# Exponentials written to the scores' PSUM bank, and scores issued after the previous pair's values and transposes

## The chip, the cores and the metric

One core of a Trainium2 chip. The metric is device time in microseconds, the median of several executions. TensorE is PE, VectorE DVE, ScalarE ACT, GpSimd POOL and SyncE SP.

## The reference

Windowed attention feeds two feed-forward blocks. q, k and v have 4 batches, 8 heads, 576 positions and 64 per head:

```python
scores = scale * np.matmul(q, k.transpose(0, 1, 3, 2))
mask = (rel >= 0) & (rel < 64)
scores = np.where(mask, scores, -1000000000.0)
attn = np.exp(scores - np.max(scores, axis=-1, keepdims=True))
attn = attn / (np.sum(attn, axis=-1, keepdims=True) + 1e-09)
x = np.matmul(attn, v)             # 2304 tokens x 512
a, b = x @ w1, x @ w2              # 512 -> 1024 each
x = (a * b @ w3) @ w_out           # -> 512
h = x @ w_in                       # 512 -> 2048
out = (h * sigmoid(h)) @ w_out2    # -> 512
```

q, k, v and the output are float32, the weights float64.

## The kernel before, in words

The kernel has three parts. The weight stage (`phase_w`, to 92 us) converts the 64-bit weights to float32 in pieces of 128x512 and multiplies w3 and w_out into one matrix (L582). A piece passes through two steps on ACT (L125, L128), two on DVE (L138, whose result `cv_z` lies in PSUM, and L141), an addition on POOL (L145), and for some a split in a high and a low part (L153 on ACT, L157 on DVE or POOL). `phase_a` runs once for each of six blocks of 384 tokens: 24 units of 12 matmuls (L618, L648), whose sums ACT copies (L632) and DVE multiplies (L634), and whose product is split again (L85, L88). The last part, from about 400 us on, is the second feed-forward block; the change does not touch it.

Attention is cut into 72 steps, here called pairs: two heads by 128 tokens. Each pair is laid over the work of the other parts in halves. `half(h)` is called between the matmuls of the weight stage (28 halves) and then once per unit of `phase_a`. Pair g goes through four even and odd halves:

- even half 2g: `scores(g)` puts the scores of both heads, 128x2x192, in one PSUM bank (tag "s", one buffer). DVE adds the mask, scales and reduces them (L344, once per head), to `sm` in SBUF. ACT then takes the exponentials (`exps`, L355, once per head) with their sums.
- odd half 2g+1: `normalise(g)` reduces the sums (L363), inverts them (L365) and multiplies (L367), all on DVE.
- even half 2g+2: `transposes(g)` (L377, three on PE into the bank "t") and their copy or split by `split_t` (L383, or L387 to L392).
- even half 2g+4: `values(g)` (L404 to L406, or L411 and L412) into the bank "o"; the parts are added in the following odd half (L419 to L423).

Pairs below 17 are "plain": one float32 matmul for scores (L329), and one copy each for transposes and values (L383, L407). The others work with high and low parts (L333, L337, L297, L303, L309, L318, L321).

Everything is in program order on each engine (the schedule is written by hand): what stands first in an engine's stream waits, and all behind it waits too. `fill()` puts steps of the weight conversion between attention's DVE instructions, so both share one queue.

The bank "s" is free for the next pair, in the kernel before, as soon as both L344 have read it. `sm` has two buffers.

Of the kernel before, what the change touches and what calls it, by code (L numbers as in the profile page):

```python
# [13 lines left out]
AF = mybir.ActivationFunctionType  # L14
ALU = mybir.AluOpType
# [27 lines left out]
def tile_window_attention_ffn(ctx, tc, qkv, qkp, vp, mask, w1, w2, w3t, w_out, w_in, w_out2, out):  # L43
# [7 lines left out]
    nc = tc.nc  # L51
# [189 lines left out]
    NG = NU * NPAIR  # L241
    LAST_HALF = 2 * NG + 4
    qk_raw, v_raw, qk_st, v_st, s_st, p_st = {}, {}, {}, {}, {}, {}
# [17 lines left out]
    def plain(g):  # L261


        return g < PLAIN
# [59 lines left out]
    def scores(g):  # L324
        s_ps = psa.tile([128, 2, 192], F32, name=f"s{g}", tag="s")
        t = qk_raw.pop(g) if plain(g) else qk_st.pop(g)
        if plain(g):
            k = t.rearrange("p (h n) -> p h n", h=2)[:, :, 0:192]
            nc.tensor.matmul(s_ps, lhsT=t[:, 192:320], rhs=k, start=True, stop=True)  # L329
        else:  # L330
            for h in range(2):

                nc.tensor.matmul(  # L333
                    s_ps[:, h], lhsT=t[:, 128 + h * 128 : 256 + h * 128],
                    rhs=t[:, 384 + h * 192 : 576 + h * 192], start=(h == 0), stop=False,
                )
            nc.tensor.matmul(s_ps, lhsT=t[:, 0:128], rhs=k_lo[g % 2], start=False, stop=True)  # L337
        nm = att.tile([128, 2], F32, name=f"nm{g}", tag="nm", bufs=2)
        rs = att.tile([128, 2], F32, name=f"rs{g}", tag="rs", bufs=2)
        fill(2)  # L340
        at = mask_at[mask_kind(place(g)[0])]
        for h in range(2):

            nc.vector.tensor_tensor_reduce(  # L344
                out=sm[g % 2][:, h, :], in0=s_ps[:, h, :], in1=consts[:, at + 64 - 64 * h : at + 256 - 64 * h],
                op0=ALU.add, op1=ALU.min, scale=-(D ** -0.5), scalar=3.0e38, accum_out=nm[:, h : h + 1],
            )
        fill()
        s_st[g] = (nm, rs)

    def exps(g):
        nm, rs = s_st[g]
        for h in range(2):
            x = sm[g % 2][:, h, :]
            nc.scalar.activation(  # L355
                out=x, in_=x, func=AF.Exp, scale=-1.0, bias=nm[:, h : h + 1], accum_out=sums_of[g % 2][:, h, 0:1]
            )

    def normalise(g):
        _, rs = s_st.pop(g)  # L360
        x = sm[g % 2]
        fill()
        nc.vector.tensor_reduce(out=rs, in_=sums_of[g % 2], axis=mybir.AxisListType.X, op=ALU.add)  # L363
        fill()
        nc.vector.reciprocal(out=rs, in_=rs)  # L365
        fill()
        nc.vector.tensor_tensor(out=x, in0=x, in1=rs.unsqueeze(2).to_broadcast([128, 2, 192]), op=ALU.mult)  # L367

    def transposes(g):

# [9 lines left out]
    def split_t(g, t_ps):  # L380
        if plain(g):
            p_st[g] = p_w[g % 2]
            nc.scalar.copy(out=p_st[g], in_=t_ps[:, 0:320])  # L383
            return
        b, a = pt[g % 2, 1], pt[g % 2, 0]
        own, before = t_ps[:, 0:256].rearrange("p (h n) -> p h n", h=2), t_ps[:, 256:320]
        nc.scalar.copy(out=b[:, :, 0, :], in_=own)  # L387
        for h, hs in HEADS:
            nc.scalar.copy(out=a[hs, h, 0], in_=before[hs])
        nc.vector.tensor_tensor(out=b[:, :, 1, :], in0=own, in1=f32(b[:, :, 0, :]), op=ALU.subtract)  # L390
        for h, hs in HEADS:
            nc.vector.tensor_tensor(out=a[hs, h, 1], in0=before[hs], in1=f32(a[hs, h, 0]), op=ALU.subtract)  # L392

    def values(g):
        u, c = place(g)
        r = u % 3 * 128

        tag = "z" if done["step"] == len(line) and g % 2 else "o"
        o_ps = psa.tile([128, 2, 2, 128], F32, name=f"o{g}", tag=tag)
        if plain(g):  # L400


            v, p, o = v_p[g % 3], p_st.pop(g), o_ps[:, 0, 0]
            nc.tensor.matmul(o, lhsT=v[:, 0:128], rhs=p[:, 0:128], start=True, stop=False)  # L404
            nc.tensor.matmul(o, lhsT=v[:, 64:192], rhs=p[:, 128:256], start=False, stop=False)
            nc.tensor.matmul(o[:, 0:64], lhsT=v[:, 192:320], rhs=p[:, 256:320], start=False, stop=True)  # L406
            return lambda: nc.scalar.copy(out=xr[:, c, r : r + 128], in_=o)  # L407
        vhl = v_st.pop(g)
        b, a = pt[g % 2, 1], pt[g % 2, 0]
        for h in range(2):  # L410
            nc.tensor.matmul(o_ps[:, h], lhsT=vhl[:, h], rhs=b[:, h], start=(h == 0), stop=False)  # L411
        nc.tensor.matmul(o_ps[:, :, :, 0:64], lhsT=vhl[:, 2], rhs=a, start=False, stop=True)  # L412
        o_ps = o_ps.rearrange("p h t n -> p h (t n)")

        def total():
            t = att.tile([128, 256], F32, name=f"ot{g}", tag="ot", bufs=1)
            if g == NG - 1:
                att.tile([128, 24], F32, name="odd_end", tag="odd_end", bufs=1)
            nc.scalar.copy(out=t[0:64], in_=o_ps[64:128, 0, :])  # L419
            nc.scalar.copy(out=t[64:128], in_=o_ps[0:64, 1, :])  # L420
            nc.vector.tensor_tensor(out=t[0:64], in0=o_ps[0:64, 0, :], in1=t[0:64], op=ALU.add)
            nc.vector.tensor_tensor(out=t[64:128], in0=o_ps[64:128, 1, :], in1=t[64:128], op=ALU.add)  # L422
            nc.gpsimd.tensor_tensor(out=xr[:, c, r : r + 128], in0=t[:, 0:128], in1=t[:, 128:256], op=ALU.add)  # L423

        return total

    def half(h):

        g, odd = divmod(h, 2)
        if not odd:
            if g < NG:
                scores(g)
            squeeze(unit_of[0])
            if 2 <= g <= NG + 1:
                sums.append(values(g - 2))
                if plain(g - 2):
                    sums.pop()()
            if 1 <= g <= NG:  # L440
                split_t(g - 1, transposes(g - 1))
            if g < NG:
                exps(g)
        else:
            if g < NG:
                normalise(g)
            if sums:
                sums.pop()()
            lows = prep_qk(g + 2)
            if g < NG:  # L450
                lows += prep_v(g)
            blk, r = divmod(g - 2, 3 * NPAIR)
            if r == 3 * NPAIR - 1 and not plain(g - 2):
                split_x(blk, 3)
            for low in lows:
                low()

            for x in range(g + 2, g + 5):
                if plain(x) and x > g + 2:
                    break  # L460
                load_qk(x)
            for x in range(g + 1, g + 4):
                if g < (x - 1 if plain(x - 3) else x - 3):
                    break
                load_v(x)
# [675 lines left out]
```

## Time and profile before

| | |
|---|---|
| median of 3 executions | 841.4 us (841.26 to 842.33) |
| profiled execution, its time | 841.24 us |
| its span | 839.5 us |
| PE, DVE, ACT, POOL busy | 827.4, 615.3, 561.2, 529.7 us |
| TensorE clock granted | 1.0 throughout |

The span is the time between the first and the last instruction that the profile shows; 1.7 us of the execution lie around it. A busy time is the sum of an engine's instructions, so an engine at 99% can have few gaps, and one at 70% can still be the one that others wait for in a stretch. The timeline gives start and duration of each instruction on each engine; "[0.71 <-DVE sm L367]" behind a row says how long the engine was idle before it and who ended that.

### The profile page before, as it was taken

The numbers are of one execution on the slowest core, as the hardware profiler recorded it, in microseconds if no ns is written. First come the engines' busy times: TensorE is split into PE (matmuls) and PEld (weight loads), VectorE is DVE, ScalarE is ACT, GpSimd is POOL, SyncE is SP. The second block draws the span as 40 slices with busy tenths as digits, with TensorE's granted clock in tenths as the row PEclk, the third lists the DMA queues.
The fourth block names the chain that finished last, engine by engine and source line by source line (L and its number), as shares of the span: only waits on it lengthen the run. The fifth ranks groups of instructions, "written<-read, shape, count | busy, mean of one in ns | idle before, by whom it ended". The sixth has DMA issues, their size and how long they took to land.

```text
span 839.5 us, 14173 instructions
## 1 busy us (share of the span) xinstructions
PE 827.4 (99%) x4418; PEld 745.9 (89%) x4418; DVE 615.3 (73%) x1424; ACT 561.2 (67%) x1390; POOL 529.7 (63%) x588
## 2 busy tenths in 40 slices
PE   7999999999999999999999999999999999999998
PEld 3555799999999999999999988888888888988986
DVE  7889877688888888888368698998644567644544
ACT  6889778898898898898556566556543446443433
POOL 5768666677777677677565577876454456454441
PEclk9999999999999999999999999999999999999999
DMA  9998234444544544543433522301301201201002
GB/s 320 330 321 279 72 107 128 149 127 133 167 150 142 169 156 145 170 157 103 155 134 120 194 76 76 125 26 51 102 26 56 95 26 64 88 25 51 1 1 75
DMA packets 54682, 102.66 MB, mean 122 GB/s; under 512 B 5200, under 2 KB 32592, under 8 KB 54608
## 3 DMA queue, kind: packets, MB, share of 16 engines
q1 hardware_dynamic: 51008, 96.91, 35.5%
q10 hardware_dynamic: 3600, 4.85, 1.6%
q8 instruction: 35, 0.57, 0.3%
q14 instruction: 39, 0.32, 0.1%
HBM read 88.11 MB, written 13.63 MB: 121 GB/s over the span
## 4 chain that ended last, share of the span: by engine, by line
PE 69%; POOL 8%; ACT 6%; issue 4%; DVE 1%; ACTq 0%; POOLq 0%; DVEq 0%
PE o L882 24%; PE ab L618 14%; PE hy L828 12%; PE hx L828 9%; PE x L648 6%; POOL klo L303 2%; POOL vhl L321 1%; ACT sm L355 1%; PE t L377 1%; POOL xr L423 1%; ACT qkhi L297 1%; POOL p L88 1%; POOL cv_b L189 1%; PE o L411 1%; PE s L333 1%
## 5 line engine op out<-in xcount | busy, mean ns | idle before, releaser
L882 PE MATMUL o<-hl,gp 128*128 128x512 f32 x504 | 133.3, 394 | 0.0
L618 PE MATMUL ab<-xa,hl 128*128 128x384 f32 x576 | 119.0, 341 | 0.0
L828 PE MATMUL hy<-xop,j 128*128 128x384 f32 x576 | 115.9, 335 | 0.0
L618 PE MATMUL ab<-xb,hl 128*128 128x384 f32 x570 | 115.2, 334 | 0.0
L88 POOL TENSOR_TENSOR gp<-tmp,gp 128x384 fp32r<-128x384 f32 x56 | 64.1, 1145 | 77.5 <-ACT gp L85 75.9
L828 PEld LDWEIGHTS hy<-xop,j 128*128 128x128 f32 x576 | 102.6, 188 | 9.0 <-DVE tmp L722 1.0
L882 PEld LDWEIGHTS o<-hl,gp 128*128 128x128 f32 x504 | 93.1, 188 | 13.1
L618 PEld LDWEIGHTS ab<-xb,hl 128*128 128x128 f32 x570 | 100.3, 188 | 0.0
L618 PEld LDWEIGHTS ab<-xa,hl 128*128 128x128 f32 x576 | 99.1, 188 | 0.0
L844 ACT ACTIVATE tmp<-hx 128x384 f32<-128x384 f32 x48 | 23.6, 492 | 111.5 <-DVE hx L722 67.8
L722 DVE TENSOR_TENSOR tmp<-hy,tmp 128x384 f32<-128x384 f32 x96 | 53.2, 554 | 56.1 <-PE hy L828 51.5
L828 PE MATMUL hx<-xop,j 128*128 128x384 f32 x432 | 86.6, 335 | 0.0
L882 PE MATMUL o<-hl,gq 128*128 128x512 f32 x324 | 85.9, 393 | 0.0
L88 POOL TENSOR_TENSOR gq<-tmp,gq 128x384 fp32r<-128x384 f32 x36 | 39.0, 1084 | 74.3 <-ACT gq L85 74.3
L828 PEld LDWEIGHTS hx<-xop,j 128*128 128x128 f32 x432 | 76.8, 188 | 4.1
L423 POOL TENSOR_TENSOR xr<-ot 128x128 f32<-128x128 f32 x55 | 32.7, 594 | 73.7 <-DVE ot L422 65.5
L303 POOL TENSOR_TENSOR klo<-qk,qkhi 64x192 fp32r<-64x192 f32 x110 | 67.2, 611 | 7.6 <-ACT qkhi L297 2.7
L882 PEld LDWEIGHTS o<-hl,gq 128*128 128x128 f32 x324 | 60.3, 188 | 11.2
L648 PE MATMUL x<-p,wp 128*128 128x384 f32 x360 | 69.6, 339 | 0.0
L355 ACT ACTIVATE sm<-sm,nm 128x192 f32<-128x192 f32 x144 | 64.5, 450 | 3.9 <-DVE nm L344 2.5
L648 PEld LDWEIGHTS x<-p,wp 128*128 128x128 f32 x360 | 61.9, 188 | 0.0
L145 POOL TENSOR_TENSOR cv_b<-cv_b,cv_r 128x512 int32<-128x512 int32 x32 | 48.6, 1520 | 18.8 <-DVE cv_b L141 9.4
(146 smaller groups left out, 1896.7 us busy)
## 6 DMA issues: line engine op xcount, KB each, us to landing
qk<-in_qkv SPq DMA_DIRECT2D x55, 384.0 KB, 3.1
words<-in_w_out SPq DMA_DIRECT2D x24, 512.0 KB, 5.4
r<-w_in SPq DMA_DIRECT2D x22, 512.0 KB, 3.4
words<-in_w3t SPq DMA_DIRECT2D x16, 512.0 KB, 6.5
words<-in_w SPq DMA_DIRECT2D x16, 512.0 KB, 6.2
xe<-in_w_in SPq DMA_DIRECT2D x16, 512.0 KB, 4.8
v<-in_qkv SPq DMA_DIRECT2D x55, 96.0 KB, 2.7
x2d<-x2s ACTq DMA_DIRECT2D x24, 192.0 KB, 1.9
```

The lines of the kernel that those rows point to most:

```text
L88: (nc.vector if eng_lo == "dve" else nc.gpsimd).tensor_tensor(out=lo, in0=src, in1=f32(hi), op=ALU.subtract)
L145: nc.gpsimd.tensor_tensor(out=x, in0=b, in1=self.r, op=ALU.add)
L189: nc.gpsimd.tensor_tensor(out=self.b, in0=self.b, in1=self.r, op=ALU.add)
L303: nc.gpsimd.tensor_tensor(out=k_lo[g % 2][hs, h * 192 : h * 192 + 192], in0=t[hs, n], in1=f32(hi[hs, n]), op=ALU.subtract)
L355: nc.scalar.activation(out=x, in_=x, func=AF.Exp, scale=-1.0, bias=nm[:, h : h + 1], accum_out=sums_of[g % 2][:, h, 0:1])
L423: nc.gpsimd.tensor_tensor(out=xr[:, c, r : r + 128], in0=t[:, 0:128], in1=t[:, 128:256], op=ALU.add)
L618: nc.tensor.matmul(acc, lhsT=w[:, l, fs], rhs=x[k // 2][:, k % 2, r, :], start=(k == 0 and n == 0), stop=(k == 3 and n == 2),)
L648: nc.tensor.matmul(acc, lhsT=wp[f][:, l, o * 128 : (o + 1) * 128], rhs=p[f][:, r, :], start=(f == 0 and n == 0), stop=(f == 7 and n == 2),)
L722: eng.tensor_tensor(out=out, in0=a, in1=b, op=op)
L828: nc.tensor.matmul(bank[name], lhsT=w[:, l, at + kt], rhs=x[:, kt, r, :], start=(fresh and kt == 0 and n == 0), stop=(kt == 1 and n == 2), ...
L844: nc.scalar.activation(out=sg, in_=src, func=AF.Sigmoid)
L882: nc.tensor.matmul(oacc[t], lhsT=g[:, l, cols], rhs=weights["out", 2 * p + i][:, r, :], start=(p == 0 and i == 0 and n == 0), stop=(p == P ...
```

## The change

`exps` writes its result to the PSUM tile of the scores, `s_ps`, in place of `sm`, and `normalise` reads it from there and writes `sm` as before. The bank "s" is thus in use until normalise has read it. So that the next pair's scores can be issued after that, an even half now has `values(g-2)`, then `transposes(g-1)`, then `scores(g)`, where it had the scores first. The calls that follow on ACT and DVE keep their order.

```diff
         fill()
-        s_st[g] = (nm, rs)
+        s_st[g] = (nm, rs, s_ps)
 
     def exps(g):
-        nm, rs = s_st[g]
+        nm, rs, e = s_st[g]
         for h in range(2):
             x = sm[g % 2][:, h, :]
             nc.scalar.activation(
-                out=x, in_=x, func=AF.Exp, scale=-1.0, bias=nm[:, h : h + 1], accum_out=sums_of[g % 2][:, h, 0:1]
+                out=e[:, h, :], in_=x, func=AF.Exp, scale=-1.0, bias=nm[:, h : h + 1], accum_out=sums_of[g % 2][:, h, 0:1]
             )
...
-        _, rs = s_st.pop(g)
+        _, rs, e = s_st.pop(g)
...
-        nc.vector.tensor_tensor(out=x, in0=x, in1=rs.unsqueeze(2).to_broadcast([128, 2, 192]), op=ALU.mult)
+        nc.vector.tensor_tensor(out=x, in0=e, in1=rs.unsqueeze(2).to_broadcast([128, 2, 192]), op=ALU.mult)
...
         if not odd:
+            if 2 <= g <= NG + 1:
+                sums.append(values(g - 2))
+            t_ps = transposes(g - 1) if 1 <= g <= NG else None
             if g < NG:
                 scores(g)
             squeeze(unit_of[0])
-            if 2 <= g <= NG + 1:
-                sums.append(values(g - 2))
-                if plain(g - 2):
-                    sums.pop()()
-            if 1 <= g <= NG:
-                split_t(g - 1, transposes(g - 1))
+            if sums and plain(g - 2):
+                sums.pop()()
+            if t_ps:
+                split_t(g - 1, t_ps)
             if g < NG:
                 exps(g)
```

PE's stream around even half 20 in the weight stage, before (s10 are the scores of pair 10, o8 and t9 the values and transposes of the pairs before it, accw the weight product):

```order
L582 MATMUL accw1_1_588<-wo_94,q_95 128x512
L329 MATMUL s10_711<-kq0_81 128x384
L404 MATMUL o8_721<-pw0_96,vp2_85 128x128
L405 MATMUL o8_721<-pw0_96,vp2_85 128x128
L406 MATMUL o8_721<-pw0_96,vp2_85 128x64
L377 MATMUL t9_726<-consts_69,sm1_78 128x128 x3
L582 MATMUL accw1_2_589<-wo_94,q_95 128x512
```

and in the change, whose lines from 435 on have a number that is higher by one:

```order
L583 MATMUL accw1_1_588<-wo_94,q_95 128x512
L404 MATMUL o8_711<-pw0_96,vp2_85 128x128
L405 MATMUL o8_711<-pw0_96,vp2_85 128x128
L406 MATMUL o8_711<-pw0_96,vp2_85 128x64
L377 MATMUL t9_715<-consts_69,sm1_78 128x128 x3
L329 MATMUL s10_719<-kq0_81 128x384
L583 MATMUL accw1_2_589<-wo_94,q_95 128x512
```

The scores moved behind the values and the transposes; all else stands where it stood.

ACT's stream around the exponentials of pair 6, with what each instruction waits for (the names are those of engines and DMA queues), before:

```order
L128 ACTIVATE cv_r<-words 128x512
L407 COPY xr<-o_490 128x128 [waits PE_49]
L383 COPY pw_97<-t_495 128x320 [waits PE_49]
L355 ACTIVATE sm_77,es_86<-sm_77,nm_486 128x192 [waits DVE_49] x2
L125 ACTIVATE cv_b<-words 128x512 [waits DMAHW1_49]
```

and in the change:

```order
L128 ACTIVATE cv_r<-words 128x512
L407 COPY xr<-o_484 128x128 [waits PE_49]
L383 COPY pw_97<-t_488 128x320 [waits PE_49]
L355 ACTIVATE s_492,es_86<-sm_77,nm_494 128x192 [waits DVE_49,PE_49]
L355 ACTIVATE s_492,es_86<-sm_77,nm_494 128x192 [waits Activation_49]
L125 ACTIVATE cv_b<-words 128x512 [waits DMAHW1_49]
```

The order on ACT is the same. Before, each exponential waits for the L344 of its own head. Now the first waits for both L344, and the second for the first, on ACT itself.

## Rows read from the trace of the kernel before

**Rows 1.** The page's first part: busy us, share of the span and instructions.

```profile
PE 827.4 (99%) x4418; PEld 745.9 (89%) x4418; DVE 615.3 (73%) x1424; ACT 561.2 (67%) x1390; POOL 529.7 (63%) x588
```

**Rows 2.** Timeline of PE, weight stage: start us, us, engine, line, operation, idle before.

```profile
78.75 0.52 PE L377 MATMUL t<-consts,sm 128*128 128x128 f32 x3 [0.71 <-DVE sm L367]
```

**Rows 3.** Timeline of DVE, weight stage: normalise.

```profile
60.35 0.56 DVE L367 TENSOR_TENSOR sm<-sm,rs 128x384 f32<-128x384 f32 x1
...
77.25 1.35 DVE L367 TENSOR_TENSOR sm<-sm,rs 128x384 f32<-128x384 f32 x1
```

**Rows 4.** Timeline of PE, steady part of attention: transposes, and one pair's scores and values.

```profile
120.95 0.49 PE L377 MATMUL t<-consts,sm 128*128 128x128 f32 x3
...
194.39 0.49 PE L377 MATMUL t<-consts,sm 128*128 128x128 f32 x3
...
230.43 0.36 PE L333 MATMUL s<-qkhi 128*128 128x192 f32 x2
...
230.82 0.39 PE L411 MATMUL o<-pt,vhl 128*128 128x256 f32 x2
...
390.65 0.52 PE L377 MATMUL t<-consts,sm 128*128 128x128 f32 x3
```

**Rows 5.** Timeline of all engines, one turn of the steady part.

```profile
232.34 0.56 DVE L634 TENSOR_TENSOR a<-ab,a 128x384 f32<-128x384 f32 x1
...
234.08 0.46 ACT L355 ACTIVATE sm<-sm,nm 128x192 f32<-128x192 f32 x1
...
234.44 0.19 ACT L355 ACTIVATION_READ_ACCUMULATOR sm<-sm,nm 128x1 f32 x1
...
234.53 0.44 ACT L355 ACTIVATE sm<-sm,nm 128x192 f32<-128x192 f32 x1
...
235.10 0.16 DVE L363 TENSOR_REDUCE rs<-es 128x2 f32<-128x4 f32 x1 [0.23 <-ACT sm L355]
235.29 0.17 DVE L365 RECIPROCAL rs<-rs 128x2 f32<-128x2 f32 x1
...
237.68 0.56 DVE L634 TENSOR_TENSOR a<-ab,a 128x384 f32<-128x384 f32 x1
```

**Rows 6.** DVE by line and shape: count, busy us, mean ns, idle before.

```profile
L367 DVE TENSOR_TENSOR sm<-sm,rs 128x384 f32<-128x384 f32 x72 | 52.5, 729 | 2.5
...
L634 DVE TENSOR_TENSOR a<-ab,a 128x384 f32<-128x384 f32 x48 | 26.8, 557 | 16.3 <-PE ab L618 10.1 <-ACT a L626 5.0
```

**Rows 7.** Timeline of POOL, weight stage: additions of the weight conversion.

```profile
60.39 1.66 POOL L145 TENSOR_TENSOR cv_b<-cv_b,cv_r 128x512 int32<-128x512 int32 x1
...
63.25 1.27 POOL L145 TENSOR_TENSOR w3x<-cv_b,cv_r 128x512 int32<-128x512 int32 x1
```

**Rows 8.** ACT by line and shape, last part: sigmoid from SBUF and from PSUM (hx).

```profile
L844 ACT ACTIVATE tmp<-tmp 128x384 f32<-128x384 f32 x48 | 25.2, 525 | 21.6 <-DVE tmp L722 21.2
L844 ACT ACTIVATE tmp<-hx 128x384 f32<-128x384 f32 x48 | 23.6, 492 | 111.5 <-DVE hx L722 67.8 <-PE hx L828 43.7
```

**Rows 9.** Timeline of all engines, weight stage: scores of pair 7.

```profile
47.01 0.81 PE L329 MATMUL s<-kq 128*128 128x384 f32 x2
...
47.66 0.39 PE L404 MATMUL o<-pw,vp 128*128 128x128 f32 x2
...
47.88 0.35 DVE L344 CUSTOM_DVE_ANT_0 sm<-s,consts 128x192 f32<-128x192 f32 x1
...
48.27 0.50 PE L377 MATMUL t<-consts,sm 128*128 128x128 f32 x3
...
49.13 0.46 ACT L355 ACTIVATE sm<-sm,nm 128x192 f32<-128x192 f32 x1
```

**Rows 10.** Timeline of ACT, weight stage: its wait for POOL.

```profile
78.22 0.62 ACT L153 CAST hl<-cv_b 128x512 fp32r<-128x512 f32 x1 [1.24 <-POOL cv_b L145]
```

**Rows 11.** Timeline of DVE and POOL, end of a block of the steady part.

```profile
218.87 1.31 DVE L367 TENSOR_TENSOR sm<-sm,rs 128x384 f32<-128x384 f32 x1
...
221.14 0.58 POOL L423 TENSOR_TENSOR xr<-ot 128x128 f32<-128x128 f32 x1 [1.38 <-DVE ot L422]
```

## The prediction

> **What bounds the kernel now.** I read the page's engine shares first: TensorE (PE) is busy for 99% of the span [rows 1]. So the time is PE's work plus its few gaps, and the change adds no PE work: three transposes, the scores and the values of each pair stay, in another order. A "pair" here is one attention step, two heads by 128 tokens; there are 72, and pair g has its scores in even half g.
>
> Next, PE's timeline for gaps. Nearly all of them stand in front of the transposes L377. Up to 118 us this happens at seven places (starts at 12.38, 19.74, 31.45, 61.05, 78.75, 84.11 and 110.14 us), together 5.5 us; one of them is [rows 2]. The reader is to see that normalise L367 of [rows 3] starts at 77.25, ends 1.35 us later at 78.60, and that the transposes start at 78.75, 0.15 after it. From 120.95 to 194.39 us PE never waits: 14 pairs in 73.44 us, 5.246 us each. From there to 390.65 us come 37 pairs in 196.26 us, where 37 x 5.246 = 194.1: 2.2 us of waits [rows 4]. So attention holds under 8 us that could be won.
>
> Who sets the pace where PE waits? In the steady part the timeline of all engines shows a loop over ScalarE (ACT) and VectorE (DVE): product L634, its split, the copies of the transposes, two exponentials, the copies L419 and L420, the sums L421 and L422, L309, and L634 again. L634 starts at 232.34 and 237.68 [rows 5]: 5.34 us, 0.09 more than PE needs, so PE's lead is eaten up by a tenth of a microsecond per pair. In the weight stage (to 92 us) ACT, DVE and GpSimd (POOL) share the bound in turn with PE.
>
> **The change part by part.**
>
> *Normalise reads PSUM.* Its 72 instructions have a mean of 729 ns, while L634, of the same shape with one input in PSUM, has 557 [rows 6]. An undisturbed L367 takes 0.56 too [rows 3]. The excess, 72 x 172 ns = 12.4 us, sits in twelve instructions that start while a POOL operation runs, such as the one of 1.35 us. The reverse happens as well: POOL's L145 takes 1.66 us when L367 starts just before it, and 1.27 otherwise [rows 7]. L634's mean shows that a form with a PSUM input is not stretched, so I take both away. [...]
>
> *Exponentials write PSUM.* No row shows ACT writing there. Two things come with it. First, ACT's rows in the new order, above, show the second exponential waiting for ACT itself, that is for the first one to be complete. Now it starts at 234.53, while the first one's accumulator read runs from 234.44 to 234.63 [rows 5]. A hand-over on one engine takes 0.03 (DVE L363 ends at 235.26, L365 starts at 235.29), so the second starts 0.13 later. Second, its own duration: the nearest rows are those that read PSUM in place of SBUF, 492 against 525 ns [rows 8]. I take these 33 ns for a write also, twice per pair, and get +0.13 - 0.066 = +0.064 us per pair on ACT. The bounds are 0.13 (nothing saved) and 0 (65 ns saved on each, twice the nearest row). [...]
>
> *The first exponential waits for both score reductions.* Before, each waited for its own. That is 0.3 us (one L344 of 0.35 less its overlap), and counts only where ACT is waiting for DVE.
>
> *Scores go behind values and transposes.* This has two prices.
> (a) The scores no longer cover a wait for normalise. In the weight stage they take 0.65 us (47.01 to 47.66, [rows 9]), in the steady part 0.39 (230.43 to 230.82, [rows 4]). PE ends that much later after a place where the transposes wait. It does not add up over places, because a PE that is late meets normalise later: it counts once, at the last such place of each stage.
> (b) Scores reach DVE later. In pair 7 scores start at 47.01 and transposes at 48.27 [rows 9]. In the new order scores stand behind the values (0.61) and three transposes (0.35 to 0.5): about 1.0 later. DVE began its reduction at 47.88, right when the scores were ready, so here it waits; behind it in its queue stand the steps of the weight conversion, and ACT's exponentials stand ahead of its own conversion steps. Where normalise's queue brings DVE to the reduction 1.2 us after normalise anyway (pairs 2, 4, 9, 12, 13, 17) it costs nothing. DVE is early in pairs 5, 6, 7, 10, 14 and 15. Worked through in turn, with PE already 0.65 late from (a) and the second reduction's 0.3, the exponentials of pairs 5, 6 and 7 come 1.0, 1.8 and 1.9 us late, and pair 10 adds 0.9. Pairs 14 and 15 have 1.8 and 1.4 us between normalise and transposes, which hides theirs.
>
> *The sum, weight stage:* +0.65 (a), +1.9 and +0.9 (b), +0.3 (five pairs at 0.064 on ACT), and the relief. POOL paces 60 to 79 us; without three stretches of 0.39 and the one at 77.25, ACT's wait of 1.24 for POOL [rows 10] goes: -1.24, no more, since ACT itself has no other gap there. Together +2.5. Bounds: -0.6 if every late reduction is absorbed (0.65 - 1.24), +3.8 without the relief.
>
> *Steady part:* +0.39 (a), +0.3 for the later reductions at its begin, where DVE has only 0.5 us to spare, and 8 pairs x 0.064 = +0.5 in the first block. Then per block of 12 pairs the loop has 12 x 0.064 = +0.77, and the relief takes 0.75 off: L367 at 218.87 takes 1.31 in place of 0.56, and L421, L422, POOL's L423 and ACT's next split follow it in a chain, with POOL idle for 1.38 [rows 11]. So the later blocks keep their pace; the steady part gives +1.2. The other stretched L367 of a block end beside an ACT that is busy anyway: nothing. Bounds from the loop: with 0 per pair the blocks gain 0.75 three times and the part gives -1.6; with 0.13 it gives +4.1.
>
> After 401 us nothing changes, and PE there runs on; the shift stays. Sum: 2.5 + 1.2 = 3.7 on the profiled execution's 841.24, which stands 0.2 below the median: **845.0 us**.
>
> **Rivals.**
> *Faster, 838.2 us.* Contention is the true pace of the weight stage. Then freeing DVE and POOL (12.4 us of DVE, 0.39 on POOL at many pairs) lets normalise of pairs 8, 11 and 12 end before PE arrives, whose waits are 0.9, 0.9 and 0.3 us; a net -1.4 there, with the conversion's gaps soaking up (b), and the loop falls to 5.25 (exponentials 65 ns shorter), -1.6. It decides if normalise of pair 12 ends at least 1 us earlier than now. For it: POOL runs without a gap from 59 to 79 us. Against: pairs 5 to 7 lie ahead of that, and there DVE waits for PE.
> *No change, 841.5.* Late reductions are absorbed to half, or the blocks' relief is larger than one chain: each takes 2 to 3 us from the sum.
> *Exponentials cost more, 848.5.* Nothing is saved by the PSUM write, and the hand-over on ACT is the full 0.13 or more: 44 pairs x 0.066 = 2.9 more. For it: no row of such a write.
> *The change does not free the port, 848.5.* L367 stays stretched: neither the 1.24 nor three times 0.75. Against: L634's 557 as a mean over 48 instructions in the same stages.
>
> **How the numbers follow.** A measurement tells 0.2%, 1.7 us, from no change: faster is below 839.7, slower above 843.1. The forecast has 0.38, dearer exponentials 0.11, the unfreed port 0.05: slower 0.54. No change 0.22, faster 0.24. The range of 838.5 to 850 leaves out the lower part of the faster case and the far end of dear exponentials, about 2 in 10. The forecast's own range is 843.1 to 848.
>
> **What would show it.** Right: L367 at 557 in mean, L145 without 1.66; in pairs 5 to 7 DVE waits for scores in front of L344, which before it hardly ever did; the second exponential starts 0.55 to 0.6 after the first, not 0.45; phase A begins 2 to 3 us later; PE waits in front of transposes in the steady part of some 3.4 us. Wrong: those waits gone there, with the loop under 5.25; or phase A begins earlier; or an L367 over 0.6.

## The result, and the profile after

The change is slower: 850.16 us (median of five runs, 847.92 to 850.79) against 842.27 us for the kernel before in the same comparison. The ratio is 1.0094, with a 95% interval of 1.0078 to 1.011. The forecast was 845.0, with a range up to 850.0: the direction was right, the size was not. The profiled run took 850.77 us, with a span of 848.9, 9.4 more than before's.

First the busy times, from the first part of the page of the changed kernel:

```profile
PE 832.1 (98%) x4418; PEld 747.8 (88%) x4418; DVE 602.4 (71%) x1424; ACT 568.7 (67%) x1390; POOL 521.0 (61%) x588
```

Against [rows 1] DVE has 12.9 us less to do and POOL 8.7 us less, and yet the kernel takes longer. No engine has an instruction more than before, so the loss is time in which engines wait for one another or run slower. PE shows both: it is busy for 4.7 us more with the same instructions, and idle for 4.7 us more (span less busy time, 12.1 us before and 16.8 now). The groups of instructions (line, engine, operation, busy us, mean ns, idle time ahead and what ended it) tell what each edit did:

```profile
L355 ACT ACTIVATE s<-sm,nm 128x192 f32<-128x192 f32 x144 | 61.1, 424 | 14.0 <-DVE nm L344 11.3
L145 POOL TENSOR_TENSOR cv_b<-cv_b,cv_r 128x512 int32<-128x512 int32 x32 | 47.2, 1474 | 25.7 <-DVE cv_b L141 10.9 <-DVE rs L365 7.0 <-DVE rs L363 4.7
L367 DVE TENSOR_TENSOR sm<-s,rs 128x384 f32<-128x384 f32 x72 | 40.1, 557 | 2.5
```

Normalise has a mean of 557 ns, as forecast (729 in [rows 6]), and POOL's addition is no longer stretched by it (1474 ns in mean, 1520 before; the longest into `q` takes 1283, before 1644). An exponential that writes PSUM takes 424 ns; into SBUF it took 450, and ACT waited 2.5 us there for the reductions L344. What is new is that it waits 11.3 us for them. The line before:

```profile
L355 ACT ACTIVATE sm<-sm,nm 128x192 f32<-128x192 f32 x144 | 64.5, 450 | 3.9 <-DVE nm L344 2.5
```

PE's timeline of the weight stage shows where this comes out:

```profile
20.08 0.87 PE L377 MATMUL t<-consts,sm 128*128 128x128 f32 x3 [3.05 <-DVE sm L367]
64.90 0.52 PE L377 MATMUL t<-consts,sm 128*128 128x128 f32 x3 [2.21 <-DVE sm L367]
83.85 0.52 PE L377 MATMUL t<-consts,sm 128*128 128x128 f32 x3 [1.96 <-DVE sm L367]
122.96 0.52 PE L377 MATMUL t<-consts,sm 128*128 128x128 f32 x3
410.47 0.49 PE L377 MATMUL t<-consts,sm 128*128 128x128 f32 x3
```

The last two rows are the transposes of pair 17 and of pair 71, the last pair. In the kernel before:

```profile
115.67 0.50 PE L377 MATMUL t<-consts,sm 128*128 128x128 f32 x3
401.04 0.49 PE L377 MATMUL t<-consts,sm 128*128 128x128 f32 x3
```

I use these two times as marks for every kernel below: up to pair 17 the change loses 7.3 us, and in the 54 pairs from there another 2.1 (287.51 us against 285.37). The marks favour the new order a little at pair 17, since the scores of pair 18 then still stand behind them: the first matmul of `phase_a` that follows starts at 123.71 in place of 115.93, 7.8 us later, which leaves 1.6 for the rest. So most of the loss is in the weight stage, where I had forecast 2.5.

The timeline of DVE and ACT at pair 6 shows one link of it:

```profile
40.64 0.36 DVE L344 CUSTOM_DVE_ANT_0 sm<-s,consts 128x192 f32<-128x192 f32 x1 [0.83 <-PE s L329]
40.92 0.35 DVE L344 CUSTOM_DVE_ANT_0 sm<-s,consts 128x192 f32<-128x192 f32 x1
41.38 0.42 ACT L355 ACTIVATE s<-sm,nm 128x192 f32<-128x192 f32 x1 [0.96 <-DVE nm L344]
41.96 0.42 ACT L355 ACTIVATE s<-sm,nm 128x192 f32<-128x192 f32 x1
```

DVE waits 0.83 us for the late scores. ACT then waits for the second reduction too, which begins at 40.92, and the second exponential begins 0.58 after the first (0.45 in [rows 5]). In the steady part, on ACT's timeline, it is 0.67:

```profile
236.24 0.42 ACT L355 ACTIVATE s<-sm,nm 128x192 f32<-128x192 f32 x1
236.68 0.20 ACT L355 ACTIVATION_READ_ACCUMULATOR s<-sm,nm 128x1 f32 x1
236.91 0.43 ACT L355 ACTIVATE s<-sm,nm 128x192 f32<-128x192 f32 x1
237.27 0.19 ACT L355 ACTIVATION_READ_ACCUMULATOR s<-sm,nm 128x1 f32 x1
237.48 0.48 ACT L633 COPY a<-ab 128x384 f32<-128x384 f32 x1
```

From the first exponential to the copy are 1.24 us, against 1.01 before (from 234.08 in [rows 5]). That is not all loss, because the first exponential also starts sooner behind the casts L389: 0.32 us after their start in place of 0.46. From the casts to the copy are 1.56 us in place of 1.47. The rows that show it, two of before and one of the change:

```profile
233.62 0.43 ACT L389 CAST pt<-t 64x64 fp32r<-64x64 f32 x2
235.09 0.48 ACT L632 COPY a<-ab 128x384 f32<-128x384 f32 x1
235.92 0.42 ACT L389 CAST pt<-t 64x64 fp32r<-64x64 f32 x2
```

One thing more had not been foreseen. The stretches after two of PE's waits have a low clock (columns: stretch, its length, busy us of PE, PEld, DVE, ACT and POOL with counts, granted clock, DMA share, GB/s). In the change:

```profile
20.00:24.00 4.00, 3.92 (x8) 2.24 (x9) 2.47 (x7) 2.83 (x9) 1.95 (x2) 0.57 1.02 381
84.00:88.00 4.00, 4.00 (x9) 1.89 (x9) 3.91 (x10) 3.29 (x11) 1.75 (x2) 0.61 0.33 90
```

Before, it is 1.00 in both. Read in steps of 1 us, the change's clock is 0.53, 0.50, 0.50 and 0.77 from 20 to 24 us and 0.95, 0.50, 0.50 and 0.50 from 84 to 88, so the mean near 0.6 comes from a clock at 0.50 for most of each stretch. PE had stood idle for 3.05 and 1.96 us just before. From the transposes of pair 11 to those of pair 12 the change takes 6.75 us (83.85 to 90.60), before took 5.36 (78.75 to 84.11).

### The profile page after: what moved, and what is told of

It reads as the page before. It is cut to its first block, busy times and chain, and to the rows that moved or that the text cites. A ratio compares the mean times of both kernels' runs of the same rounds, so it can differ in the third digit from the quotient of the medians.

```text
span 848.9 us, 13869 instructions
## 1 busy us (share of the span) xinstructions
PE 832.1 (98%) x4418; PEld 747.8 (88%) x4418; DVE 602.4 (71%) x1424; ACT 568.7 (67%) x1390; POOL 521.0 (61%) x588
## 4 chain that ended last, share of the span: by engine, by line
PE 66%; ACT 16%; DVE 6%; issue 4%; ACTq 0%; POOL 0%; DVEq 0%
PE o L883 24%; PE hy L829 12%; PE ab L619 10%; PE hx L829 9%; PE x L649 6%; ACT s L355 5%; PE accw L583 2%; DVE a L635 2%; ACT pt L389 2%; DVE ot L422 1%; ACT ot L420 1%; ACT a L633 1%; ACT ot L419 1%; PE t L377 1%; ACT p L85 1%
## 5 line engine op out<-in xcount | busy, mean ns | idle before, releaser
L619 PE MATMUL ab<-xa,hl 128*128 128x384 f32 x576 | 116.5, 336 | 0.0
L619 PEld LDWEIGHTS ab<-xa,hl 128*128 128x128 f32 x576 | 101.7, 188 | 0.8
L355 ACT ACTIVATE s<-sm,nm 128x192 f32<-128x192 f32 x144 | 61.1, 424 | 14.0 <-DVE nm L344 11.3
L145 POOL TENSOR_TENSOR cv_b<-cv_b,cv_r 128x512 int32<-128x512 int32 x32 | 47.2, 1474 | 25.7 <-DVE cv_b L141 10.9
```

Of the source, the lines that this page charges most:

```text
L145: nc.gpsimd.tensor_tensor(out=x, in0=b, in1=self.r, op=ALU.add)
L355: nc.scalar.activation(out=e[:, h, :], in_=x, func=AF.Exp, scale=-1.0, bias=nm[:, h : h + 1], accum_out=sums_of[g % 2][:, h, 0:1])
L619: nc.tensor.matmul(acc, lhsT=w[:, l, fs], rhs=x[k // 2][:, k % 2, r, :], start=(k == 0 and n == 0), stop=(k == 3 and n == 2),)
```

## The experiments

Three theories stood at the start. *Order*: the late scores, which no longer cover PE's waits either. *Write*: what the write to PSUM adds around the exponentials, that is the wait for both reductions ("both-wait") and the second exponential's wait for the first ("hand-over"). *Clock*: the two slow stretches.

All results together. "Pair 17" is the start of its transposes, "later" the time from there to the transposes of pair 71; both are from the profiled run, the ratio and its interval from all runs. Each ratio is to the kernel before in the same comparison (medians of 841.2 to 842.27). Between a kernel of before's order and one of the new order, add 0.5 to the loss at pair 17 and take it off the later one, for the reason given above.

| kernel | median us | ratio to before | pair 17 | later |
|---|---|---|---|---|
| before | 842.27 | 1 | 115.67 | 285.37 |
| the change | 850.16 | 1.0094 [1.0078, 1.011] | 122.96 | 287.51 |
| order_alone | 844.27 | 1.0033 [1.002, 1.0046] | 118.85 | 284.56 |
| both_wait | 847.44 | 1.0073 [1.0061, 1.0086] | 119.81 | 286.12 |
| hand_over | 858.65 | 1.0206 [1.0192, 1.022] | 120.09 | 298.21 |
| write_old_order | 853.48 | 1.0133 [1.0118, 1.0149] | 126.83 | 288.68 |
| weight_stage_only | 847.42 | 1.0072 [1.006, 1.0085] | 121.76 | 285.36 |
| busy_waits | 850.27 | 1.0102 [1.0088, 1.0116] | 121.69 | 287.70 |
| reciprocal_in_psum | 837.40 | 0.9955 [0.9943, 0.9968] | 114.14 | 282.99 |
| own_bank | 848.89 | 1.0085 [1.0071, 1.0099] | 115.42 | 292.02 |
| one_values_bank | 847.62 | 1.0076 [1.0059, 1.0093] | 115.90 | 291.57 |
| free_port_order | 841.94 | 1.0004 [0.9995, 1.0013] | 117.69 | 284.29 |
| free_port_both_wait | 843.57 | 1.0025 [1.0015, 1.0034] | 120.49 | 283.84 |
| free_port_hand_over | 849.70 | 1.0096 [1.0081, 1.0111] | 119.16 | 289.42 |
| free_port_both_wait_and_hand_over | 852.34 | 1.0125 [1.011, 1.014] | 123.29 | 289.04 |
| free_port_old_order_hand_over | 845.55 | 1.005 [1.0035, 1.0065] | 117.45 | 288.53 |

### The order by itself

The change, with exponentials and normalise back in SBUF:

```diff
-        s_st[g] = (nm, rs, s_ps)
+        s_st[g] = (nm, rs, sm[g % 2])
```

> The new order (values, transposes, scores), with the exponentials and the normalise in SBUF as before. Theory order: the late scores and the lost cover carry the loss, so this is as slow as the whole change or slower, since normalise is stretched again: 848 to 852 us, accw after pair 12 at 90 us or later (84.5 before, 91.6 with the change), VectorE waits for scores in front of L344 as with the change (some 16 us up to 125 us). Theory write: the loss is in the exponentials that write PSUM, and the order costs only the cover, 0.65 and 0.39 us: 843 to 845 us, accw after pair 12 at 85 to 86 us.

Measured: +2.8 us by the ratio, a third of the whole loss; pair 17 is 3.2 us later. The reductions do wait for scores, as theory order has it (DVE waits 5.1 us for scores of L329, the change 5.4), but the change has 4.1 us more by pair 17. The write is the larger part.

### The write by itself, in before's order

```diff
-            if 2 <= g <= NG + 1:
-                sums.append(values(g - 2))
-            t_ps = transposes(g - 1) if 1 <= g <= NG else None
             if g < NG:
                 scores(g)
             squeeze(unit_of[0])
+            if 2 <= g <= NG + 1:
+                sums.append(values(g - 2))
...
+            t_ps = transposes(g - 1) if 1 <= g <= NG else None
```

> The exponentials in the scores' PSUM bank, with the scores first in a pair as before. The bank then comes free only when normalise has read it, so scores, values and transposes all stand behind that wait. Theory order: what costs is that scores cannot cover the wait; here they do not either, and the values lose their place ahead of it as well, so it is slower than the whole change, by up to 0.6 us at each place where PE waits: 851 to 855 us. Theory write: the order matters little and this is within 1.5 us of the whole change, 848.5 to 851.5 us.

Measured 853.48, the time that theory order gave. Scores now stand at the head of the pair and wait for normalise to leave their bank (from PE's waits up to 125 us):

```profile
PE s L329 <- DVE sm L367: 3.4, 1, 3.4
PE s L329 <- ACT cv_b L125: 2.2, 1, 2.2
PE s L329 <- ACT hl L153: 2.1, 1, 2.1
```

The last two lines name ACT. There the scores start at 65.54 and 86.39, and normalise had to leave their bank as well; which of the two came last PE's rows don't show. The profiled run took 855.75 us and has a low clock from 20 to 24 us (0.50) and from 86 to 90 (0.65), and slow transposes at 66.98 (0.85 us, as at 88.17), so its marks are later than the median would give. Given the write, then, the reorder is worth its price: 853.48 falls to 850.16 (ratios 1.0133 and 1.0094, intervals apart). It pays back part of a cost that the write brought in.

### Only in the weight stage

`g < 14` chooses the change's order (in `half`) and bank; later pairs have before's.

```diff
-        s_st[g] = (nm, rs, s_ps)
+        s_st[g] = (nm, rs, s_ps if g < 14 else sm[g % 2])
```

> The whole change for pairs 0 to 13 (up to some 105 us), before's order and SBUF from pair 14 on. By the two traces the change loses 7.1 us by the begin of phase A, 7.7 by pair 17 and 9.4 at the end. If the two parts add, this gives 842.3 + 7 to 7.7 = 849 to 850 us. If a late weight stage is made up for later (before's waits in front of the transposes of pairs 14 to 17, 1.4 to 1.8 us, go when PE is late anyway), it gives 846 to 848 us.

Measured 847.42: by the ratio 6.1 us lost, all of it by pair 17 (+6.1), with before's pace behind it (285.36 against 285.37). So the stages add, and a late weight stage is not made up for. It is below the 849 to 850 expected. In the profiled run the clock is one reason: it had a granted clock of 1.00 from 84 to 88 us, after nearly the same wait (1.97 us), and went from pair 11 to pair 12 in 5.34 us (84.23 to 89.57) where the change took 6.75.

### PE kept busy in the two waits ahead of the low clock

```diff
         x = x.rearrange("p h n -> p (h n)")
+        for _ in range({1: 4, 11: 3}.get(g, 0)):
+            nc.tensor.matmul(t_ps, lhsT=idle_in[:, 0:128], rhs=idle_in[:, 0:384], start=True, stop=True)
```

> The whole change, with four matmuls of 0.65 us that nobody reads in front of the transposes of pair 1, where PE waits 3.05 us, and three in front of those of pair 11, where it waits 1.96 us; both waits were followed by a granted clock near 0.6. Theory clock: 3.4 of the loss is the two stretches of some 4 us at the lower of the clock's levels; granted clock 1.00 in 20 to 24 and 84 to 88 us, accw after pair 12 at 88 to 88.5 us in place of 91.6, total 846.5 to 847.5 us. Rival: the pace is set by ACT, DVE and POOL, and a faster PE only waits longer at the next transposes; total 849.5 to 851 us with the clock at 1.00. The spread of the runs speaks for the rival: one with a mean clock of 1.0 took 849.61.

The same two stretches now:

```profile
20.00:24.00 4.00, 3.45 (x11) 1.91 (x12) 2.94 (x8) 3.44 (x9) 2.52 (x2) 1.00 1.02 354
84.00:88.00 4.00, 4.00 (x13) 2.06 (x13) 3.91 (x10) 3.36 (x11) 1.84 (x2) 1.00 0.30 76
```

The clock holds, and the median doesn't move: 850.27 against 850.16. Of the 3.4 us that I ascribed to the clock, 1.3 are gained at pair 17, 1.1 at pair 71 (409.39), and none in the medians. PE's timeline tells why for the first stretch: it comes out of it sooner, and waits longer at the next transposes it has to wait for, 1.70 us at 32.77 in place of 0.70 at 32.69. There PE isn't what sets the pace. In the second stretch it is: pair 12 comes 5.43 us after pair 11 (83.85 to 89.28) in place of 6.75, and this is the 1.3 us that is still there at pair 17. So theory clock falls as the main cause. The second stretch costs 1.3 us of the 7.3 in the profiled run of the change; how much of that is in its median these runs don't show, since they lie between 847.92 and 850.79.

### The two waits of the write, one by one

Both are put on order_alone, without any write to PSUM. The first:

```diff
         nm, rs, e = s_st[g]
-        for h in range(2):
+        for h in (1, 0):
```

> The order alone (exponentials and normalise in SBUF), with the second head's exponential issued first. It waits for the second reduction, and so for both, as the write to PSUM makes the first exponential do; no hand-over is added, since the other one then waits for nothing. The order alone took 2.8 us, the whole change 7.9: the write adds 5.1. Theory both-wait: up to 92 us ACT waits 8.6 us for L344 with the change and 5.3 us with the order alone, and these 3.3 us are most of it: 847 to 848 us, ACT's wait for L344 near 8 us up to 92 us, accw after pair 12 at 89 to 90.5 us (87.3 with the order alone, 91.6 with the change). Theory hand-over: within 1 us of the order alone, 843.5 to 845 us.

The second, where one column gets its exponential twice:

```diff
-            x = sm[g % 2][:, h, :]
+            x = sm[g % 2].rearrange("p h n -> p (h n)")[:, 191 * h : 192 + 192 * h]
...
-                out=e[:, h, :], in_=x, func=AF.Exp, scale=-1.0, bias=nm[:, h : h + 1], accum_out=sums_of[g % 2][:, h, 0:1]
+                out=x, in_=x, func=AF.Exp, scale=-1.0, bias=nm[:, h : h + 1], accum_out=sums_of[g % 2][:, h, 0:1]
```

> The order alone, with the second exponential taking one column of the first head along (193 columns). So it needs the first one complete, as two writes to one PSUM bank do; the first waits for its own reduction only. That column gets its exponential twice. Theory hand-over: 14 pairs by 0.14 us are 2.0 us in the weight stage, where ACT shares the bound, and 0.06 to 0.09 a pair later on: 846.5 to 848 us; second exponential 0.57 to 0.67 us after the first, accw after pair 12 at 89 to 90 us. Theory both-wait: ACT's own 0.14 is hidden in its waits, 844 to 845 us.

The first gives 3.4 us (from 1.0033 to 1.0073). ACT's exponentials up to 92 us, by line, for order_alone, both_wait and the change:

```profile
L355 ACT ACTIVATE sm<-sm,nm 128x192 f32<-128x192 f32 x28 | 12.5, 448 | 5.4 <-DVE nm L344 5.3
```

```profile
L355 ACT ACTIVATE sm<-sm,nm 128x192 f32<-128x192 f32 x28 | 12.6, 452 | 8.2 <-DVE nm L344 8.0
```

```profile
L355 ACT ACTIVATE s<-sm,nm 128x192 f32<-128x192 f32 x26 | 11.0, 425 | 9.0 <-DVE nm L344 8.6
```

So the wait for both reductions brings ACT's wait from 5.3 to 8.0, near the change's 8.6. But pair 17 is only 1.0 later, not the 2 to 3 expected.

The second gives 14.6 us by the ratios, several times what theory hand-over asked for and more than the whole change loses. Most of it falls into the later part (298.21). The profile tells why; in the steady part, on POOL and DVE:

```profile
237.33 1.28 POOL L189 TENSOR_TENSOR cv_b<-cv_b,cv_r 128x512 int32<-128x512 int32 x1
237.41 1.62 DVE L367 TENSOR_TENSOR sm<-sm,rs 128x384 f32<-128x384 f32 x1
```

Normalise was pushed to just behind a POOL operation and is stretched to 1.62 us; its mean rose to 864 ns, from 687 in order_alone. The change's normalise reads PSUM and is not stretched (557). Hence SBUF is the wrong ground for this test, and I looked for one where normalise is free.

### The port freed without any write

"The port" is short here for whatever makes normalise and POOL's operations hold each other up when normalise has both inputs in SBUF. The traces show the stretching, not the part of the chip. On the kernel before, the reciprocals (128x2) go into free columns of the transposes' bank. Exponentials and order stay:

```diff
-        _, rs = s_st.pop(g)
+        s_st.pop(g)
         x = sm[g % 2]
+        t_of[g] = psa.tile([128, 512], F32, name=f"t{g}", tag="t")
+        rs = t_of[g][:, 384:386]
...
-        t_ps = psa.tile([128, 384], F32, name=f"t{g}", tag="t")
+        t_ps = t_of.pop(g)
```

> Before's order and before's exponentials in SBUF; only the sums and reciprocals that normalise multiplies by (128x2) go into free columns of the transposes' PSUM bank, so that normalise has one input in PSUM and nothing is moved. Theory contention: L367 falls to a mean near 560 ns and L145 to near 1474 as with the change, and as no price is paid for it, the weight stage gains 1 to 2 us and the loop of the later pairs 0.75 in a block: 838 to 840 us. Rival, contention is hidden: both means fall but ACT and PE keep their pace, 841 to 842 us. Third: an input of two columns in PSUM doesn't free the port, L367 stays over 650 ns: 841 to 842.5 us.

Measured 837.40, 3.8 us faster than before by the ratio; by the two ratios (0.9955 and 1.0094) the change is 11.7 us above it. Normalise, the exponentials and the addition on POOL, by line:

```profile
L356 ACT ACTIVATE sm<-sm,nm 128x192 f32<-128x192 f32 x144 | 64.5, 450 | 3.9 <-DVE nm L345 2.5
L145 POOL TENSOR_TENSOR cv_b<-cv_b,cv_r 128x512 int32<-128x512 int32 x32 | 46.7, 1461 | 19.8 <-DVE cv_b L141 10.8 <-DVE t L368 4.6 <-DVE t L366 3.1
L370 DVE TENSOR_TENSOR sm<-sm,t 128x384 f32<-128x384 f32 x72 | 39.9, 553 | 2.5
```

Two columns in PSUM free normalise (553 ns) as well as the whole input does, and ACT's wait for reductions stays at before's 2.5. Pair 17 gains 1.5 us and the later part 2.4. From pair 12 to the end the timeline marks no wait of PE in front of the transposes any more:

```profile
83.07 0.52 PE L380 MATMUL t<-consts,sm 128*128 128x128 f32 x3
392.07 0.52 PE L380 MATMUL t<-consts,sm 128*128 128x128 f32 x3
397.13 0.49 PE L380 MATMUL t<-consts,sm 128*128 128x128 f32 x3
```

### The change rebuilt, piece by piece, without the write

On that kernel the pieces are put back: the order, then each wait, then both. In the two kernels with the hand-over one column gets its exponential twice.

```diff
+            if 2 <= g <= NG + 1:
+                sums.append(values(g - 2))
+            t_ps = transposes(g - 1) if 1 <= g <= NG else None
             if g < NG:
                 scores(g)
...
```

> The kernel with the reciprocals in PSUM (837.4 us, normalise not stretched, exponentials in SBUF), with the change's order: values, transposes, scores. It is the change without the exponentials' write. If what the order costs adds to what the free port gives: 837.4 + 2.8 = 840.2 us, accw after pair 12 at 85.5 to 87 us. If the cover was what hid the stretched normalise, the order costs less here: 838 to 839.5 us.

> As free_port_order, with the second head's exponential first, so that the first one issued waits for both reductions. Theory both-wait: 3.3 us as without the free port, some 843.5 us, ACT's wait for L345 up to 92 us near 8 us. Rival: in SBUF the 3.3 us came from stretched normalises that it moved on to; with the port free it costs under 1 us, 840 to 841 us.

> As free_port_order, with the second exponential taking one column of the first head along, so that it needs the first one complete. In SBUF this took 14 us, 1.1 of it in the weight stage and the rest where normalise fell behind POOL's operations (mean 911 ns up to 400 us). Theory: with the port free that amplification is gone, and what is left is 0.12 us a pair where ACT sets the pace: 841.5 to 844 us, loop 5.44 to 5.46 us. Rival: the loop itself is the cost, 40 pairs by 0.12 and more: 848 us or above.

free_port_both_wait and free_port_hand_over add the lines shown for both_wait and hand_over. For both waits, the loop goes over `(1, 0)` and the exponential over this slice:

```diff
+            x = sm[g % 2].rearrange("p h n -> p (h n)")[:, 192 * h : 384 - 191 * (1 - h)]
```

> Both waits together on free_port_order: the order, the free port, the wait for both reductions and the hand-over, but the exponentials still in SBUF. If these four are the whole mechanism of the change, it comes to the change's time, 848 to 852 us, with the first accw after pair 12 at 90 to 92.5 us (91.6 with the change). If something of the PSUM write itself is missing (a conflict in the bank, the read of it by normalise), it stays below 847 us.

By the ratios the order costs 4.1 us here (0.49% of 841.5), the wait for both reductions 1.8 on top of it, the hand-over 7.7, and both waits 10.2. Up to pair 17 that is 3.55, 2.80, 1.47, and 5.60 for both: 1.3 more than the two alone. The clock accounts for as much: like the change, the last kernel had the low clock from 84 to 88 us (0.69), behind PE's wait of 1.92 us, and it takes 6.74 us from pair 11 to pair 12. free_port_order, both single waits and weight_stage_only, with 1.00 there, take 5.34 to 5.40. Without it the two waits come to 4.3 us by pair 17, the sum of the two alone. The 2.80 of free_port_both_wait contains a low-clock stretch of its own (0.57 from 20 to 24 us) and slow matmuls behind (eight into accw take 5.16 us from 65.15, four take 1.88 from 71.75), and free_port_order a low clock from 20 to 24 us (0.63), so the split between the two waits is rough.

The last kernel follows the change through the weight stage. Its rows in PE's timeline (pairs 11, 12, 16 and 17):

```profile
84.22 0.52 PE L380 MATMUL t<-consts,sm 128*128 128x128 f32 x3 [1.92 <-DVE sm L370]
90.96 0.50 PE L380 MATMUL t<-consts,sm 128*128 128x128 f32 x3
117.68 0.52 PE L380 MATMUL t<-consts,sm 128*128 128x128 f32 x3 [0.77 <-DVE sm L370]
123.29 0.52 PE L380 MATMUL t<-consts,sm 128*128 128x128 f32 x3
```

and the change's own:

```profile
83.85 0.52 PE L377 MATMUL t<-consts,sm 128*128 128x128 f32 x3 [1.96 <-DVE sm L367]
90.60 0.50 PE L377 MATMUL t<-consts,sm 128*128 128x128 f32 x3
117.35 0.52 PE L377 MATMUL t<-consts,sm 128*128 128x128 f32 x3 [0.83 <-DVE sm L367]
122.96 0.52 PE L377 MATMUL t<-consts,sm 128*128 128x128 f32 x3
```

They run 0.3 to 0.4 us apart, with nearly the same waits. So the order, a freed normalise, the two waits and the low clock behind one of PE's waits are the mechanism of the weight stage, and no conflict in the PSUM bank is needed to explain it. The median of 852.34 stands just above the 848 to 852 expected; the excess is in the later part (289.04 against 287.51), where the exponentials into SBUF are longer (0.46 us each, 0.42 to 0.43 in the change).

### The hand-over in before's order, and a run that told nothing

own_bank gives the exponentials the bank "z" and the values the bank "o" alone:

```diff
-        s_st[g] = (nm, rs)
+        e = sm[g % 2]
+        if done["step"] == len(line):
+            e = psa.tile([128, 2, 192], F32, name=f"e{g}", tag="z")
+        s_st[g] = (nm, rs, e)
...
-        tag = "z" if done["step"] == len(line) and g % 2 else "o"
+        tag = "o"
```

> Before's order throughout; from the pair on at which the weight conversion is done (some 17), the exponentials go into a PSUM bank of their own, which half of the values' accumulators gave up, and normalise reads it. Scores stay first and wait for nothing. The later part of the change lost 1.7 us. Theory hand-over: the loop over ACT is 0.09 longer (5.42 to 5.43 in place of 5.335), 12 times in a block, less 0.75 of relief: 842 to 843.5 us. Rival, the late scores and the wait for both reductions cost the later part: without them the relief is left, 839.5 to 841 us.

one_values_bank has the last two lines alone:

> The kernel before with one bank for the values' sums throughout (own_bank without the exponentials' write). own_bank ended 6.4 us after before at the last transposes, and its values waited for that single bank in every pair. If the bank is what cost: 847 to 849 us. If the hand-over between the exponentials is: 841 to 842.5 us, with the loop at 5.335 us, since the bank then comes free as early as PE comes to it.

own_bank was meant to show the write without late scores, but to find a bank it took one from the values. The control takes 847.62, and its later part 291.57 against own_bank's 292.02. So the bank explains that run, neither theory on own_bank does, and it says nothing on the write.

The better test is the hand-over (the slice of hand_over, one column twice) on the kernel with the freed port, in before's order:

> The kernel with the reciprocals in PSUM, before's order, with the second exponential needing the first one complete (one column shared). On the new order this took 1.5 us up to pair 17 and 5.1 us later. If the hand-over is ACT's own cost in the loop, the later part loses the same 5 us here (transposes from pair 17 to 71 in 287.5 to 289 us, 283.0 without it) and the whole 843 to 845.5 us. If it costs only where the scores come late, 838 to 840 us.

It costs 8.0 us by the ratios (0.9955 to 1.005): 3.3 by pair 17 and 5.5 later. So the hand-over doesn't need the late scores. Its rows on ACT, and DVE's product that closes the loop:

```profile
236.61 0.46 ACT L356 ACTIVATE sm<-sm,nm 128x192 f32<-128x192 f32 x1
236.97 0.19 ACT L356 ACTIVATION_READ_ACCUMULATOR sm<-sm,nm 128x1 f32 x1
237.19 0.46 ACT L356 ACTIVATE sm<-sm,nm 128x193 f32<-128x193 f32 x1
```

```profile
234.89 0.56 DVE L637 TENSOR_TENSOR a<-ab,a 128x384 f32<-128x384 f32 x1
240.34 0.56 DVE L637 TENSOR_TENSOR a<-ab,a 128x384 f32<-128x384 f32 x1
```

The second exponential starts 0.58 after the first, and the loop has 5.45 us in place of 5.34 in [rows 5].

## Why the prediction was wrong

**Right: normalise.** I forecast 557 ns and that the stretching of POOL would end. Both happened (the stretched ones before were fifteen, not twelve; the 12.4 us of excess is right). Alone, reciprocal_in_psum shows, this is worth 1.5 us by pair 17 (forecast 1.24) and 2.4 later (three times 0.75). With an input in PSUM normalise takes 557 and 553 ns in these two kernels, and 0.56 us undisturbed with both in SBUF [rows 3].

**Right: the order.** (a) and (b), the lost cover and the late reductions, were 0.65 + 1.9 + 0.9 = 3.45 us in the weight stage. order_alone measures 3.2 by pair 17 and free_port_order 3.55, each 0.5 more when counted behind the scores. Part of that agreement is luck: the 1.9 contained 0.3 for the second reduction, for which these two kernels do not wait, and 1.0 of order_alone's 3.2 comes at pair 16 (PE waits 1.06 us there in place of 0.33), behind the weight stage for which the sum was made.

**Wrong: "The first exponential waits for both score reductions" and "five pairs at 0.064 on ACT".** The first stood in the sum only inside the 0.3 of a second reduction, on the ground that it counts only where ACT is waiting for DVE, and the second as +0.3. Together 0.6; measured on free_port_order they are 5.6 by pair 17, of which 1.3 is the low clock behind the wait of PE at pair 11. My rule for when the first counts was right, but I applied it to the waits of the trace of before, 2.5 us up to 92 us. The same change makes the scores late, and with them ACT waits for DVE in a dozen pairs (waits of ACT, us in total, times, longest, up to 125 us):

```profile
ACT s L355 <- DVE nm L344: 10.5, 12, 1.9
```

I should have priced the second edit on the timeline that the first one leaves.

**Wrong: the hand-over's size.** I took +0.13 for it and 0.033 off each exponential, 0.064 per pair. The hand-over itself was 0.13: in the weight stage the second exponential starts 0.58 after the first in place of 0.45. Each exponential saved 0.026, not 0.033. In the steady part the second starts 0.67 after the first, and the read of the first one's accumulator 0.44 after its start in place of 0.36, but the first exponential also starts 0.14 sooner behind L389, so that 0.09 per pair is left on ACT. The loop has 5.42 to 5.43 us (the product L635 starts at 240.07 and 245.49), 0.08 to 0.09 more than in [rows 5]. The later part lost 2.1 us by the marks, or 1.6 behind the scores, where I forecast 1.2. That is a size within its bounds.

**Missing: the clock.** Its fall was not foreseen, and no term stood for it. The stretch behind the wait at pair 1 costs nothing that lasts (pair 11 starts at 83.85 with it and, in busy_waits, without it); the one behind the wait at pair 11 costs 1.3 us by pair 17 in the profiled run, though busy_waits doesn't show a gain in its median.

**The rivals.** "Exponentials cost more" named the right part and 848.5 us, but looked for the cost in 44 later pairs; the 5.6 us by pair 17 are the larger part. "Faster, 838.2" is near what the freed port gives by itself: 837.4, without the write and without the new order; with the order 841.94. "The change doesn't free the port" falls with the 557 ns. The range ended 0.2 us below the median: its upper end took the dear exponentials in, but no further price for them in the weight stage. One reading of the trace of before was also off, without a part in the sum: the waits at the seven places up to 118 us are 4.4 us by the ends of PE's rows, not 5.5.

Left open: how far the wait for both reductions and the hand-over can be told apart in the change itself. Neither was taken out of it, since the two heads share one bank; they were shown by adding them elsewhere. In the later part the stand-in in SBUF is dearer than the write: from pair 17 on the change loses 3.2 us against free_port_order (284.29), the rebuilt kernel 4.75.

## What to carry to other kernels

When an operand is moved to PSUM to end a stretching like normalise's (729 ns in mean before, 557 in the change), look at what the move ties together: here the second write to the bank waited for the first, and the first for both reductions that read the bank, though the two heads share no column. End it with the smallest operand that will do; here two columns did what 384 did (553 and 557 ns), and 837.4 us stands against 850.2. When a change has two edits that delay the same chain, price the second on the timeline that the first leaves, not on the trace of before.

## What the runs showed of the hardware

- Normalise with a two-column input in PSUM takes 553 ns, as short as with its 384-column input there (557), while with both in SBUF its mean was 729, and fifteen that started beside a POOL operation took 0.85 to 1.64 us.
- An exponential of 128x192 takes 424 ns into PSUM and 450 into SBUF. The read of its accumulator starts some 0.36 us after its own start in both, except after the first exponential of each pair in the steady part of the change (0.43 to 0.44); why, these runs don't show.
- The second exponential starts 0.45 us after the first when the two share nothing, and 0.58 when it has to wait for it, as much with one shared column in SBUF as in one PSUM bank in the weight stage.
- After waits of PE of 1.92 to 4.11 us its granted clock sometimes fell, to a mean of 0.50 to 0.69 over the next 4 us stretch, and sometimes not: 1.00 from 84 to 88 us in weight_stage_only after 1.97, and 1.00 from 20 to 24 us in free_port_hand_over after 3.40.
